# Pacing the first loads of the output projection, and moving operand sums, in a transformer block on one NeuronCore

## The chip, the cores and the metric

The kernel runs on one core of one Trainium2 chip. The metric is the device time of one execution in microseconds. "Before" is the kernel as it stood, "after" the changed one. Single executions of one program scatter by up to 0.6%, so small differences are read from ratios over several rounds and, inside one profile, from the length of stages.

## The reference, cut to what matters

An adaLN modulation is made from `c` and `w_mod`; then an attention block with recurrent memory rows, then an MLP with shifted channels:

```python
mod = (_silu(c) @ w_mod).reshape(c.shape[0], 6, 1, -1)          # sa, ca, ga, sb, cb, gb
h = _layernorm(x) * (1 + ca) + sa
x = x + ga * _A_ref(h, A_mem0, A_Wq, A_Wk, A_Wv, A_Wo, A_seg_len)
h = _layernorm(x) * (1 + cb) + sb
x = x + gb * _B_ref(h, B_w1, B_w2, B_w3, B_w4)
# _A_ref: 32 heads of 128 over 2048 tokens; each segment of 32 tokens sees itself and 8 memory rows;
#         o = p @ v; out = o @ Wo; the memory rows of one segment's output feed the next segment
# _B_ref: u = gelu(layernorm(x) @ w1), shifted along the tokens; x1 = x + shifted @ w2
#         out = x1 + gelu(layernorm(x1) @ w3) @ w4
```

## The kernel before

Six names stand for the engines: in this kernel PE does the matrix products, DVE, ACT and POOL do the element-wise work, and SP, like POOL and ACT, issues DMA transfers. The kernel runs in stages: an **opening** (modulation, first layer norm, means `hbar` of the segments), the **attention** over pairs of heads, the **Wo phase** (`o @ Wo`), the **w1 and w2 tiles**, and twice, for two halves of the tokens ("pairs"), a **w3 stage** and a **w4 stage**. Large products use sums and differences of operand quarters (a fast matrix product with fewer multiplications), made on DVE. A scheduler in the compiler chooses each engine's order; `keep_order` pins an instruction behind the one written before it on that engine.

The eight sums of the opening, free to be placed:

```python
S1, S2, S4 = (hsp.tile([P, 4, CH], F16, name=f"hs{j}{p}")[:] for j in (1, 2, 4))
nc.vector.tensor_tensor(S1, A21, A22, ALU.add)
nc.vector.tensor_tensor(S2, S1, A11, ALU.subtract)
nc.vector.tensor_tensor(S4, A12, S2, ALU.subtract)
nc.vector.tensor_tensor(f16(A21), A11, A21, ALU.subtract)
```

The first loads of the Wo phase, on POOL's queue and on SP's. A unit is 32 matmuls with one 1 MB weight tile (`wstream`) and, on its first use, one 1 MB tile of attention output (`OTc`):

```python
for j in range(1, 3):
    W0_load(0, j, nc.gpsimd)
    load_ot(j, nc.gpsimd)
for t, src in RW:
    nc.gpsimd.dma_start(t[:], src.partition_broadcast(P))
...
interleave(att[done:], ... + W0[0][0] + W0[0][1])
load_ot(3)
...
for j in range(4, 6):
    load_ot(j)
```

The w2 tiles: PE fills a PSUM bank, DVE empties it (`x1b`), ACT takes the squares, three small POOL steps give `ln_ve`, `ln_rstd` and `ln_nmr`, ACT normalises into `z`, and SP transposes `z` into `z2a` or `z2b` by DMA. The sums for w3 stand behind tile 14:

```python
def Bb(t):
    return lambda: nc.sync.dma_start_transpose(z2s[t // 8][:, :, ...], zs[t][:])

for i, u in enumerate(lagged(Ba, Bb, list(range(NTT)), lag=1)):
    u()
    if i in (4, 8):
        load_upto(ring_ctr[0])
    if i == 14:
        for f in z_sums(0):
            keep_order(f())
        w3_sums(0, keep_order)
LT2.close()            # the memory of z, x1b and u is free for what comes next
```

The start of the w3 stage. `snap` copies a bank on ACT, `join` adds a bank and a snap on DVE, `gelu` writes `hq` on ACT. The pools below grow downward into memory that earlier stages gave back:

```python
hq_p = RF.enter_context(tc.tile_pool(name="x3_h", bufs=1, side="right"))
...
st2 = RF.enter_context(tc.tile_pool(name="x3_s2", bufs=2, side="right"))
stm = RF.enter_context(tc.tile_pool(name="x3_sm", bufs=4, side="right"))   # join tiles
rsq = RF.enter_context(tc.tile_pool(name="x3_rq", bufs=2, side="right"))
...
for q in prod("b", A11, B11, True):
    st[q]["s1"] = snap(stA, st[q]["b"])
for q in prod("e", A12, B21, True):
    join(0, 0, q, "e", "s1")
for q in prod("b", S2, T2, False):
    st[q]["s2"] = snap(st2, st[q]["b"])
```

## Time and profile before

| | before |
|---|---|
| time, median of 3 runs | 1491.64 us |
| span of the profile | 1488.7 us |
| PE busy | 1422.2 us, 96% |
| DVE, ACT, POOL busy | 60%, 46%, 25% |

PE is the engine that is always wanted, so the profile is read as a list of PE's waits and of the stretches where its clock is low. A line of the waits is: waiting engine and line, what ended the wait, total us, how often, longest. A line of the order of work ("timeline") is: start in us, duration, engine, line, operation, output<-input, shapes, count, and in brackets the idle time before it with what ended it.

### The profile page before, as it was taken

Reading aid. Unit: us, or ns where it says so; the run is one execution under the profiler, and the core shown is the slowest. Engines: PE = TensorE matmul, PEld = TensorE weight load, DVE = VectorE, ACT = ScalarE, POOL = GpSimd, SP = SyncE. Lnnn points to the kernel's source line nnn. Section 1 sums busy time; section 2 is a strip of 40 time slices with the busy share of each in tenths; the row PEclk is TensorE's granted clock in tenths of the full one; section 3 lists DMA queues with packets and bytes.
Section 4 is the critical chain, followed back from the end, with each engine's and each line's share of the span. In section 5 each row is a group of like instructions: output and inputs, shape, how many; then the busy total and the mean of one; then the engine's idle time right before and its main releaser. Section 6 shows DMA issues by size and latency. Waiting matters only on the chain.

```text
span 1488.7 us, 24706 instructions
## 1 busy us (share of the span) xinstructions
PE 1422.2 (96%) x9198; PEld 754.4 (51%) x9254; DVE 898.1 (60%) x1946; ACT 685.3 (46%) x1443; POOL 379.1 (25%) x530
## 2 busy tenths in 40 slices
PE   5899999999999999999997999999998999999998
PEld 3465555555555555555553444444443444444443
DVE  5517776777677777667651254353255668776684
ACT  2715666665666665666551031122566661046400
POOL 8403100000000000000010132123023557645525
PEclk9999999999999999999999999999999999999999
DMA  9687968867677787778579899994399675387812
GB/s 307 203 284 157 189 155 184 200 146 175 163 175 175 185 165 174 160 163 187 114 178 337 280 319 345 329 261 141 82 311 247 214 249 184 116 248 250 284 39 78
DMA packets 402613, 303.48 MB, mean 204 GB/s; under 512 B 199082, under 2 KB 354730, under 8 KB 400690
## 3 DMA queue, kind: packets, MB, share of 16 engines
q1 hardware_dynamic: 363632, 238.05, 60.8%
q0 software_dynamic: 9616, 33.05, 7.2%
q10 hardware_dynamic: 29234, 30.71, 6.5%
q8 instruction: 74, 1.21, 0.4%
q14 instruction: 57, 0.47, 0.1%
HBM read 200.56 MB, written 50.63 MB: 169 GB/s over the span
## 4 chain that ended last, share of the span: by engine, by line
PE 78%; DMA 5%; DVE 5%; issue 4%; POOL 3%; ACT 3%; ACTq 0%; SPq 0%; DVEq 0%; POOLq 0%
PE acc L623 29%; PE acc L895 7%; PE bank_b L1275 6%; PE bank_b L1224 6%; PE acc L1052 4%; PE acc L328 3%; PE bank_d L1224 3%; PE acc L1151 3%; PE acc L318 3%; PE bank_e L1275 2%; PE bank_d L1275 2%; PE ps_o L734 2%; DMA wstream<-in_A_Wo_dram 2%; PE ps_s L717 2%; PE bank_e L1224 1%
## 5 line engine op out<-in xcount | busy, mean ns | idle before, releaser
L895 PE MATMUL acc<-wstream,OTc 128*128 128x512 bf16 x940 | 209.1, 381 | 6.5 <-DMA OTc<-OTx_d 4.8
L623 PEld LDWEIGHTS <-T 128*128 128x128 f16 x1408 | 130.6, 97 | 119.6 <-issue 2.2
L591 ACT COPY snap<-acc 128x480 f32<-128x480 f32 x264 | 146.3, 565 | 87.3 <-PE acc L623 80.8
L623 PE MATMUL acc<-hh,T 128*128 128x480 bf16 (+1 forms) x704 | 163.1, 366 | 0.3 <-DVE VT L595 0.3
L623 PE MATMUL acc<-hs,T 128*128 128x480 f16 x704 | 157.2, 366 | 0.7 <-ACT snap L591 0.6
L895 PEld LDWEIGHTS <-OTc 128*128 128x128 bf16 x960 | 93.7, 98 | 117.9 <-DMA OTc<-OTx_d 5.0
L762 POOL DMA_DIRECT2D OTx_d<-OT x32 | 24.8, 776 | 427.6 <-DMA OT<-O 368.9
L1224 PEld LDWEIGHTS <-ring 128*128 128x128 f16 (+1 forms) x784 | 77.2, 99 | 104.2 <-issue 12.7
L721 ACT ACTIVATE E<-ps_s 99x495 bf16<-99x495 f32 (+2 forms) x160 | 87.5, 547 | 47.9 <-PE ps_s L717 47.4
L623 PE MATMUL acc<-hh,wq 128*128 128x480 bf16 x464 | 103.9, 366 | 0.0
L741 DVE TENSOR_TENSOR O<-ps_o,rin_all 99x384 bf16<-99x384 f32 (+1 forms) x192 | 97.1, 509 | 3.7
L1078 DVE TENSOR_TENSOR ring<-ring 128x1024 f16<-128x1024 bf16 (+1 forms) x64 | 85.6, 1357 | 5.3 <-PE bank_b L1275 4.8
L1275 PEld LDWEIGHTS <-hq 128*128 128x128 bf16 (+1 forms) x560 | 54.8, 98 | 66.1
L595 DVE TENSOR_TENSOR KT<-acc,snap 128x480 bf16<-128x480 f32 x116 | 74.9, 654 | 21.3 <-PE acc L623 18.7
L734 PE MATMUL ps_o<-V,E 99*128 99x129 bf16 (+1 forms) x704 | 79.8, 220 | 8.1 <-DMA V<-VT 5.5
L1189 ACT COPY snap<-bank_b 128x512 f32<-128x512 f32 x72 | 40.4, 583 | 99.4 <-PE bank_b L1275 60.3
L734 PEld LDWEIGHTS <-E 99*128 99x128 bf16 (+1 forms) x704 | 56.5, 98 | 46.0 <-issue 6.6
L993 ACT ACTIVATE u<-x,ln_nmr,ln_rstd 128x1024 bf16<-128x1024 f32 x16 | 19.7, 1231 | 128.6 <-DVE ln_nmr L992 126.4
L723 DVE TENSOR_TENSOR E<-E,maskB 99x495 bf16<-99x495 bf16 (+1 forms) x128 | 48.2, 376 | 48.4 <-ACT E L721 46.4
L739 ACT ACTIVATE O<-ps_o,rin_all 99x128 bf16<-99x128 f32 x192 | 56.7, 369 | 36.8 <-DVE rin_all L736 36.4
L736 DVE RECIPROCAL rin_all<-ps_o 99x3 f32<-99x3 f32 (+2 forms) x256 | 42.7, 171 | 50.5 <-PE ps_o L734 49.8
L1275 PE MATMUL bank_b<-ring,hq 128*128 128x512 f16 (+1 forms) x334 | 73.1, 379 | 0.1
(245 smaller groups left out, 2549.4 us busy)
## 6 DMA issues: line engine op xcount, KB each, us to landing
wstream<-in_A_Wo_dram SPq DMA_DIRECT2D x29, 1024.0 KB, 9.5
OTx_d<-OT POOLq DMA_DIRECT2D x32, 512.0 KB, 7.0
wstream<-in_B_w_dram SPq DMA_DIRECT2D x28, 512.0 KB, 5.9
ring<-in_B_w_dram SPq DMA_DIRECT2D x28, 512.0 KB, 6.4
ring<-in_B_w_dram SPq DMA_DIRECT2D x8, 1792.0 KB, 10.3
OTc<-OTx_d SPq DMA_DIRECT2D x12, 1024.0 KB, 8.8
wq<-in_A_Wq_dram SPq DMA_DIRECT2D x16, 512.0 KB, 5.1
wk<-in_A_Wk_dram SPq DMA_DIRECT2D x16, 512.0 KB, 8.0
```

The source lines that it names most:

```text
L591: nc.scalar.copy(t[:], st[q][bank][:, 0:CH])
L595: nc.vector.tensor_tensor(view(d, i), chunks(st[q][bank]), chunks(st[q][s_]), ALU.add)
L623: nc.tensor.matmul(acc[:, 0:CH], lhsT=B[:, k, :], rhs=A[:, k, :], start=(j in (1, 2, 5) and k == 0), stop=(k == 3), skip_group_check=True)
L721: nc.scalar.activation(E[:rows, 0:o], ps[:rows, 0:o], ACT.Exp, scale=DH ** -0.5)
L734: nc.tensor.matmul(ps[:, i, :], lhsT=state["e", h, t // 5][:k, c:c + P], rhs=V[:k, t, 0:DH + 1], start=True, stop=True)
L739: nc.scalar.mul(O[:rows, t, :], ps[:rows, i, 0:DH], rin[:, i:i + 1])
L741: nc.vector.tensor_tensor(O[:rows, ts[0]:ts[0] + n, :], ps[:rows, 0:n, 0:DH], rin[:, :, None].to_broadcast([rows, n, DH]), ALU.mult)
L895: nc.tensor.matmul(accs[tt][:], lhsT=ot[hl // 4][:, hl % 4, tt * P:(tt + 1) * P], rhs=woc[hl // 4][:, hl % 4, :], start=(h == 0), stop=(h ...
L1052: nc.tensor.matmul(acc[:], lhsT=w1s[:, kt, ct * P:(ct + 1) * P], rhs=zT[:, kt, b * 512:(b + 1) * 512], start=(kt == 0), stop=(kt == KT - 1))
L1078: return nc.vector.tensor_tensor(dst, a, b, op)
L1224: nc.tensor.matmul(acc[:], lhsT=B[:, k, q * P:(q + 1) * P], rhs=A[:, k, :], start=(start and k == 0), stop=(k == 3), skip_group_check=True)
L1275: nc.tensor.matmul(acc[:], lhsT=L3[:, k, i * P:(i + 1) * P], rhs=R3[:, k, :], start=(start and k == 0), stop=(k == 13), skip_group_check=True)
```

## The change

Its intent is threefold, and I name the parts for the rest of the text.

- **Sums part**: the eight sums of the opening are pinned behind it, off the path to `hbar`.
- **Wo part**: the first loads of the Wo phase go to SP, each released by a named matmul ("paced"); the memory-row transposes of the last two heads go to ACT's queue.
- **z part**: the seven sums in front of the w3 stage are spread, two per w2 tile from tile 10.

```diff
-            nc.vector.tensor_tensor(S1, A21, A22, ALU.add)
+            keep_order(nc.vector.tensor_tensor(S1, A21, A22, ALU.add))
 ... (the same for the other three sums)
+        def pace(ld, mm):
+            if mm is not None:
+                tc.add_manual_dep(ld.ins, mm.ins.name, ...)      # ld waits for matmul mm
 ...
-        for j in range(1, 3):
-            W0_load(0, j, nc.gpsimd)
-            load_ot(j, nc.gpsimd)
-        for t, src in RW:
-            nc.gpsimd.dma_start(t[:], src.partition_broadcast(P))
+        W0_load(0, 1)
+        load_ot(1)
+        paced[0, 0] = [lambda mm: W0_load(0, 2, mm), lambda mm: load_ot(2, mm)]
+        paced[0, 1] = [lambda mm: W0_load(1, 0, mm)]
+        paced[0, 2] = [lambda mm: W0_load(1, 1, mm), ... the row broadcasts RW ...]
+        paced[1, 0] = [lambda mm: W0_load(1, 2, mm), lambda mm: load_ot(3, mm)]
 ... (three more)
         for h in range(H - 2, H):
-            nc.vector.tensor_copy(ots[3][1][:, h % 8 - 4, :], ...)      # moved to a later place
+            nc.scalar.dma_start_transpose(state["mt", h][:], Os[h % 2][96:112, :, :]...)
+            keep_m(h)
 ...
-            if i == 14:
-                for f in z_sums(0):
+            if i == 10:
+                zu = z_sums(0) + w3_sums(0)
+            if i >= 10:
+                for f in zu[2 * (i - 10):2 * (i - 9)]:
                     keep_order(f())
-                w3_sums(0, keep_order)
```

The other edits of the diff, in the w3 and w4 stages, issue the same instructions in the same order.

## The prediction

> **What bounds the kernel now.** I read the page first, then the waits of PE, then the table of stretches around the three longest stalls, then the order of work there on SP and DVE.
>
> ```profile
> PE 1422.2 (96%) x9198; PEld 754.4 (51%) x9254; DVE 898.1 (60%) x1946; ACT 685.3 (46%) x1443; POOL 379.1 (25%) x530
> ```
>
> PE is busy 1422.2 of 1488.7 us. All that a change of order can win is the 66.5 us of PE's idle time, plus whatever PE loses at a lower clock after an idle. So the waits of PE are the list to go by (columns: total us, times, longest):
>
> ```profile
> PE acc L477 <- DVE hbar L465: 5.4, 1, 5.4
> PE bank_b L1224 <- ACT snap L1189: 5.1, 2, 3.2
> PE acc L895 <- DMA OTc<-OTx_d: 4.8, 1, 4.8
> PE acc L895 <- DMA wstream<-in_A_Wo_dram: 4.7, 1, 4.7
> PE bank_b L1224 <- POOL ln_rstd L1135: 4.3, 1, 4.3
> ```
>
> Four of the five lie where the diff works: the hbar wait (opening), both L895 waits (start of the Wo phase), and the last (from the w2 tiles to the w3 stage). The snap waits are not touched: the edits in the w3 and w4 stages issue the same instructions in the same order. The table of stretches (length, busy us by engine, PEclk, DMA share, GB/s) shows what a stall costs beyond itself:
>
> ```profile
> 790.00:794.80 4.80, 0.01 (x1) 0.00 (x0) 0.86 (x3) 0.34 (x1) 0.10 (x1) 1.00 1.00 249
> 794.80:798.50 3.70, 3.65 (x13) 1.63 (x14) 0.00 (x0) 0.00 (x0) 1.68 (x5) 0.55 1.02 389
> 811.60:816.20 4.60, 0.00 (x0) 0.00 (x0) 0.00 (x0) 0.00 (x0) 0.00 (x0) 0.94 1.00 276
> 816.20:818.00 1.80, 1.54 (x4) 0.66 (x6) 0.00 (x0) 0.00 (x0) 0.00 (x0) 0.50 1.27 331
> 1131.00:1135.30 4.30, 0.00 (x0) 0.01 (x1) 4.30 (x7) 2.37 (x3) 1.65 (x4) 0.74 1.05 276
> 1135.30:1141.00 5.70, 5.68 (x16) 2.12 (x17) 1.24 (x4) 4.46 (x6) 1.40 (x4) 0.60 0.92 220
> ```
>
> The stretch after each stall has a granted clock of 0.50 to 0.60. At 1131 PE does nothing while DVE is busy for all 4.30 us. On SP, the order of work around the first two stalls is:
>
> ```profile
> 778.13 0.81 SPq L861 DMA_DIRECT2D OTc<-OTx_d  x2
> 782.49 1.25 SPq L779 DMA_TRANSPOSE MT<-O  x1
> 784.41 0.45 SPq L878 DMA_DIRECT2D wstream<-in_A_Wo_dram  x1
> 784.90 10.21 SPq L861 DMA_DIRECT2D OTc<-OTx_d  x1
> 795.16 1.58 SPq L878 DMA_DIRECT2D wstream<-in_A_Wo_dram  x1
> 801.97 11.89 SPq L779 DMA_TRANSPOSE MT<-O  x1
> ```
>
> The two loads at 778.13 are for later blocks, and at 784.90 and 801.97 SP stands for 10.21 and 11.89 us at one issue. On DVE at the third stall:
>
> ```profile
> 1129.80 0.68 DVE L1153 SCALAR_TENSOR_TENSOR x1b<-acc,u 128x512 f32<-128x512 f32 x1
> ...
> 1133.82 0.69 DVE L1078 TENSOR_TENSOR ring<-ring 128x1024 f16<-128x1024 bf16 x1
> 1134.42 0.68 DVE L1153 SCALAR_TENSOR_TENSOR x1b<-acc,u 128x512 f32<-128x512 f32 x1
> ```
>
> PE's last w2 matmul ends near 1131.0, but its bank is emptied only at 1134.42 (L1153): the operand sums (L1078) stand in front. PE starts w3 at 1135.32, just after that.
>
> **What the Trainium skill says.** (1) "TensorE: Matmul & The Clock Gate", "What's actually happening": after an idle window of about 3.4 us the array runs at half rate, and back at full rate only after about 3.4 us of sustained work. The trace agrees: 8 matmuls after the idle at 790 take 3.35 us, against 1.89 us elsewhere, while the wait of 1.28 us at 123.30 shows no slow matmuls. (2) "DMA: Bandwidth & Descriptors", "Issuing engines are not separate DMA queues": transfers issued from POOL, SP and ACT share the same 16 engines and interleave. The trace agrees: the urgent POOL loads take 16.8 (weights) and 19.4 us (OTc) to land at a DMA share of 1.0, while the weight preloads at 750 (0.5 MB each) landed in 3.3 us. (3) "VectorE: DVE Perf Modes", "The perf-mode tier table": a two-operand bf16 op on 2048 elements takes 1224 ns. The trace has 1218 to 1226 ns (L1078); so 1 us a sum is not to be reduced by order, only moved.
>
> **Part 1, paced Wo loads, transposes off SP.** Before, nearly 10 MB are requested between 778 and 796: for (0,1) and (0,2) 4 MB by POOL; by SP OT 4 and 5 (2 MB), OT 3 (0.75 MB), two weight tiles (2 MB); by POOL the 1 MB of row broadcasts. At some 300 GB/s (stretches: 249 to 389) that is over 30 us, all sharing. What PE needs first at 790 is only 2 MB. After: weight tile 1 and OT 1 go first on SP at about 778 (their memory comes free then, as now), some 2.5 MB with the small loads, so about 8 us, landed by 787, 3 us ahead of 790. Tile 2 and OT 2 start when the first group of 8 matmuls ends (about 783), 2 MB more, due by 793, needed at about 797 (a unit is 32 matmuls of 0.216 us, 6.9 us). The next weight starts near 792, needed at 804. From then each unit brings 1 to 2 MB, with a lead of nearly two units, 12 to 13 us, against a median landing of 9.5 us. So both waits should go.
> - Waits: 4.84 + 4.72 = 9.6 us.
> - Clock: 3.7 x 0.45 = 1.7 us after the first, 1.8 x 0.50 + 22 x 0.02 (PEclk 0.98 from 818 to 840) = 1.3 us after the second.
> - Sum: -12.6 us. The transposes, now on ACT, sit in a stretch with 0.64 us of ACT work in 50 us: no cost on PE's path. PE is busy 49.7 of 50 us in most later stretches, so what is won here carries through, if DMA allows (rivals).
>
> **Part 2, sums over the w2 tiles.** 4 sums of 1.22 us and 3 of 0.69 us move from behind tile 14 to tiles 10 to 13. A tile is 16 matmuls, 3.45 us on PE; DVE's own work in it is 2 x (0.69 + 0.08) + 0.31 = 1.85 us. Six tiles leave 6 x 1.6 = 9.6 us for 7.0 us of sums. The first sum must wait for the last z2a transpose: issued 1111.45, landing 5.1 us (median), 1116.5. DVE then runs late by about 4 us near 1122 and has caught up by tile 15 at about 1130. Eight PSUM tiles give PE 13.8 us of slack meanwhile. The last bank is then emptied from about 1131.1 to 1131.8; PE resumes near 1132.1.
> - Wait 4.3 to 1.1: -3.2 us. Too short to lose the clock: 5.7 x 0.40 = -2.3 us.
> - Given back: ACT has tile 15's normalisation (1.13 and 1.24 us) in front of the first snaps, about +0.5.
> - Sum: -5.0 us.
>
> **Part 3, eight sums behind the opening.** Seven of them (1.15 us each) run now between 63.7 and 71.7 among the steps of hbar, on which PE waits until 73.26. Without them the chain is still held by ACT until 69.43; from there five short steps (0.34 to 0.54 us), 0.15 and 0.20 end at about 72.3: -0.9 us. The wait stays above 3.4 us, so the slow start (0.59 from 73.3 to 79.5) stays. Against it, eight sums at 1.07 us of pitch now stand on DVE from about 114 to 122.7, where the T sums (8 x 0.36 us) and the first masks (at 121.41 now) also want it. The masks may come 3 to 4 us later, when PE has other matmuls for part of that: I put +1.2 us, between 0 and 3. Sum: +0.3 us.
>
> **Total.** -12.6 - 5.0 + 0.3 = -17.3 us; 1491.6 - 17.3 = 1474.3. I hold back about 1 us for new short waits: **1475 us**.
>
> **Rivals.** (a) DMA becomes the bound of the Wo phase: its share is 1.03 to 1.06 from 850 to 1000 at 304 to 343 GB/s. If that is true saturation, PE running 12 us ahead meets loads that land later. For it: the share. Against: no wait on a load in 840 to 1020, 4 weight buffers (20.7 us of lead when not paced) against landings of 9.5 median and 16.7 at most, and a share of 0.40 in 1000 to 1050 that can take deferred stores. It would give back 4 to 10 us: 1479 to 1485. (b) The pacing is too late: a load is released only by a matmul, and a landing of 16.7 us would beat a lead of 13. Each miss costs up to 3 us, perhaps with the clock: 1478 to 1482. (c) The releaser named at 1135, POOL ln_rstd, is the true one and not the emptied bank; it would come only at about 1133, and part 2 wins 3 us instead of 5: 1477. (d) The DVE block at 114 to 123 stalls PE for over 3 us and costs the clock as well: 1479. (e) The hbar chain shortens below 3.4 us, since the compiler's order on ACT changes too: up to 3.5 us more, 1471.
>
> **Range and chances.** Most rivals cost; the two that could add are (e) and smaller waits around 750 to 800. So 1468 to 1484. 2% is 29.8 us, nearly half of all idle time of PE and more than all the touched waits with their clock (19.3 + 7.8 = 27): faster by over 2% 0.03, slower 0.01, within 0.96.
>
> **What would show it.** In the profile after: no L895 wait on OTc or wstream of over 1 us and PEclk 1.0 from 785 to 840; no SP issue that stands for 10 us there; the last L1153 within 1 us of PE's last w2 matmul and PE resuming about 1 us after it at full clock; the hbar wait at about 4.5 us. Wrong would be: new L895 waits after 830 (a or b), a wait on L1135 that stays (c), PE idle in 114 to 130 beyond the present 3 us (d).

## The result, and the profile after

The kernel after takes **1490.25 us** (median of 4 fast runs, 1486.28 to 1491.87) against 1491.89 us for the kernel before beside it (1491.34 to 1493.24). The ratio is 0.9984, with a 95% interval of 0.9963 to 1.0004: the same within 2%. A ratio is the mean time of one kernel's runs over that of the other's of the same rounds, so it is not quite the ratio of the medians quoted. Executions over 1.5% slower than the fastest of the same kernel are left out of the means. The class was predicted, but the time was not: 1475 us was predicted, with 1468 to 1484 as range. About 15 us of gain are missing.

The page of the kernel after, engine totals:

```profile
PE 1423.4 (96%) x9198; PEld 754.6 (51%) x9254; DVE 895.3 (60%) x1946; ACT 685.7 (46%) x1443; POOL 371.8 (25%) x526
```

PE is busy 1.2 us longer, so nothing was won on its idle time either. The waits of PE, after:

```profile
PE bank_b L1244 <- ACT snap L1209: 7.8, 4, 3.4
...
PE acc L477 <- DVE hbar L465: 4.6, 1, 4.6
PE ps_o L734 <- DVE O L741: 4.0, 1, 4.0
PE acc L905 <- DMA OTc<-OTx_d: 3.3, 1, 3.3
PE acc L905 <- DMA wstream<-in_A_Wo_dram: 2.4, 2, 1.8
...
PE bank_b L1244 <- POOL ln_ve L1152: 1.9, 1, 1.9
```

All four waits that the prediction aimed at became shorter: hbar 5.4 to 4.6, the Wo loads 9.5 to 5.7 together, the last one 4.3 to 1.9. But a wait of 4.0 on O is new, and the waits on snap grew from 5.1 to 7.8.

To see where the time went, I measure from the trace when PE starts the first matmul of each stage (of the w2 tiles also the last). The table gives the lengths between these marks in us, for before, after and the four runs that the argument leans on most:

| stretch | before | after | Wo part alone | Wo part, broadcast late | z part alone | best version (best2) |
|---|---|---|---|---|---|---|
| start to the first matmul of L328 (`acc<-hh,wq`, 199 columns) | 113.2 | 111.9 | 112.2 | 112.1 | 112.1 | 112.8 |
| to the first product `hs,wk` | 35.6 | 37.9 | 35.9 | 35.7 | 35.7 | 35.4 |
| rest of the attention | 632.1 | 634.5 | 632.3 | 634.2 | 634.2 | 632.1 |
| Wo phase | 239.4 | 233.0 | 231.2 | 226.5 | 240.0 | 226.5 |
| w1 and w2 tiles | 110.3 | 110.3 | 110.3 | 110.3 | 110.3 | 110.3 |
| last w2 matmul to the first w4 matmul | 93.6 | 94.8 | 95.1 | 95.1 | 94.5 | 87.8 |
| rest | 264.5 | 266.2 | 266.3 | 266.0 | 266.5 | 264.9 |

The z part alone has the same instruction order as before up to the w2 tiles, and yet its attention took 634.2 against 632.1 us: differences of 2 us in that row are scatter of single executions. After won 6.4 us in the Wo phase where 12.6 were predicted, lost 2.3 us in the second row and 1.2 us in the w3 row, and the rest is in rows that scatter.

**The new wait on O.** The order of work on DVE, before:

```profile
123.89 0.56 DVE L741 TENSOR_TENSOR O<-ps_o,rin_all 104x384 bf16<-104x384 f32 x1
...
130.30 0.43 DVE L566 TENSOR_TENSOR T<-wk,wq 128x512 f16<-128x512 bf16 x1 [3.77 <-DMA wk<-in_A_Wk_dram]
```

The same on DVE, after, and then PE, after:

```profile
124.47 0.62 DVE L595 TENSOR_TENSOR VT<-acc,snap 128x480 bf16<-128x480 f32 x1
129.22 0.43 DVE L566 TENSOR_TENSOR T<-wk,wq 128x512 f16<-128x512 bf16 x1 [4.12 <-DMA wk<-in_A_Wk_dram]
...
130.23 0.55 DVE L741 TENSOR_TENSOR O<-ps_o,rin_all 104x384 bf16<-104x384 f32 x1
```

```profile
130.84 0.51 PE L734 MATMUL ps_o<-V,E 99*128 99x129 bf16 x3 [3.96 <-DVE O L741]
```

Both times DVE stands about 4 us for a weight load of the next head pair (L566). Before, the first head's O (L741) had been done by then and nobody waited. After, the pinned sums fill DVE until 123.1 us, the scheduler put L741 behind L566, and PE waits with DVE: the load's delay, hidden before, is now on the path. The wait costs more than its length, since over the next 5 us PE's granted clock is 0.70.

**The Wo phase.** PE's longer waits there, after, then SP and POOL:

```profile
804.60 7.08 PE L905 MATMUL acc<-wstream,OTc 128*128 128x512 bf16 x32 [3.27 <-DMA OTc<-OTx_d]
820.38 16.56 PE L905 MATMUL acc<-wstream,OTc 128*128 128x512 bf16 x74 [1.79 <-DMA wstream<-in_A_Wo_dram]
```

```profile
786.88 2.87 SPq L871 DMA_DIRECT2D OTc<-OTx_d  x1
...
795.59 4.58 SPq L871 DMA_DIRECT2D OTc<-OTx_d  x1
```

```profile
781.47 0.56 POOL L1055 DMA_DIRECT2D gb_b<-rows_d  x1 [6.23 <-PE acc L328]
```

And POOL before:

```profile
796.09 0.54 POOL L1035 DMA_DIRECT2D gb_b<-rows_d  x1
```

The waits at the first use of tile 1 and at 816 us are gone. But one unit later PE waits 3.27 us for tile 2's `OTc`, and two units after that 1.79 us for a weight tile. SP still stands at its issues, though up to 825 us for 4.58 us at most where it stood for 11.89, and a 0.5 MB broadcast, `gb_b`, which is needed only in the w3 stage, is now issued at 781.47 us, in front of most urgent loads; before, it came at 796.09 us, because POOL's queue held its own urgent loads first.

**The start of the w3 stage.** PE after, and then DVE after and DVE before:

```profile
1129.96 1.89 PE L1244 MATMUL bank_b<-z2a,ring 128*128 128x512 bf16 x8 [1.95 <-POOL ln_ve L1152]
1136.93 1.46 PE L1244 MATMUL bank_b<-zs,ring 128*128 128x512 f16 x4 [3.36 <-ACT snap L1209]
1139.39 1.87 PE L1244 MATMUL bank_b<-zs,ring 128*128 128x512 f16 x4 [1.00 <-ACT snap L1209]
...
1313.87 2.62 PE L1244 MATMUL bank_b<-zs,ring 128*128 128x512 f16 x8 [3.25 <-ACT snap L1209]
```

```profile
1142.22 1.29 DVE L1252 TENSOR_TENSOR join<-bank_e,snap 128x512 f32<-128x512 f32 x2 [12.02 <-DMA z2b<-z]
```

```profile
1144.01 1.29 DVE L1232 TENSOR_TENSOR join<-bank_e,snap 128x512 f32<-128x512 f32 x2 [7.43 <-PE bank_d L1224]
```

PE starts w3 at full clock and sooner, as predicted: 2.4 us after its last w2 matmul (1127.6) against 4.7 before (1130.6). Then it waits 3.36 and 1.00 us for snaps. And DVE shows what nobody had asked about: the first join starts 14.6 us after the last w2 matmul, against 13.4 before. Its releaser after is named as a transpose of z, which a join does not read. The profiles of w_only and a_dep, whose code there is that of before, name it too.

### The profile page after: what moved, and what is told of

Same layout as the page of the kernel before. It is cut to its first block, busy times and chain, and to the rows that moved or that the text cites. A ratio compares the mean times of both kernels' runs of the same rounds, so it can differ in the third digit from the quotient of the medians.

```text
span 1488.6 us, 24703 instructions
## 1 busy us (share of the span) xinstructions
PE 1423.4 (96%) x9198; PEld 754.6 (51%) x9254; DVE 895.3 (60%) x1946; ACT 685.7 (46%) x1443; POOL 371.8 (25%) x526
## 5 line engine op out<-in xcount | busy, mean ns | idle before, releaser
L741 DVE TENSOR_TENSOR O<-ps_o,rin_all 99x384 bf16<-99x384 f32 (+1 forms) x192 | 97.1, 509 | 3.7
L595 DVE TENSOR_TENSOR VT<-acc,snap 128x480 bf16<-128x480 f32 x90 | 58.0, 650 | 24.9 <-PE acc L623 20.9
L1248 ACT ACTIVATE hq<-join 128x512 bf16<-128x512 f32 x84 | 52.8, 630 | 41.7 <-DVE join L1252 41.7
```

The costliest lines, as they stand in the source:

```text
L595: nc.vector.tensor_tensor(view(d, i), chunks(st[q][bank]), chunks(st[q][s_]), ALU.add)
L741: nc.vector.tensor_tensor(O[:rows, ts[0]:ts[0] + n, :], ps[:rows, 0:n, 0:DH], rin[:, :, None].to_broadcast([rows, n, DH]), ALU.mult)
L1248: nc.scalar.activation(hq[a][f][:, g * 2 + q, :], src[:], ACT.Gelu_apprx_tanh)
```

## The experiments

Eighteen kernels ran, all correct. They ran with 5 rounds each, in groups that share the runs of the kernel before.

| run | what it is | median us | ratio to before | 95% interval |
|---|---|---|---|---|
| a_only | sums part alone | 1492.06 | 1.0003 | 0.9982 to 1.0023 |
| w_only | Wo part alone | 1483.14 | 0.9935 | 0.9919 to 0.9951 |
| z_only | z part alone | 1492.78 | 1.0002 | 0.9986 to 1.0018 |
| wz | Wo and z parts | 1485.81 | 0.9958 | 0.9938 to 0.9979 |
| w_nomt | Wo part, transposes left on SP | 1481.62 | 0.9939 | 0.9923 to 0.9955 |
| w_mt | only the transposes moved | 1489.86 | 0.9997 | 0.9979 to 1.0014 |
| w_lean | Wo part, gb_b late | 1477.92 | 0.9917 | 0.9900 to 0.9933 |
| a_dep | sums tied behind hbar only | 1491.32 | 1.0006 | 0.9990 to 1.0022 |
| lean_adep | w_lean and a_dep | 1479.59 | 0.9906 | 0.9892 to 0.9920 |
| z_late | z part, tiles 12 to 15 | 1493.20 | 1.0014 | 1.0000 to 1.0027 |
| wz_zact | wz, ACT's normalisation pipelined | 1485.52 | 0.9966 | 0.9951 to 0.9981 |
| z_mem | z_only, join tiles moved | 1504.86 | 1.0099 | 1.0081 to 1.0117 |
| wz_zact_mem | wz_zact, join tiles moved | 1489.76 | 0.9995 | 0.9978 to 1.0013 |
| b_mem2 | before, join tiles moved, POOL pinned | 1490.64 | 0.9985 | 0.9972 to 0.9998 |
| wz_zact_mem2 | wz_zact with the same | 1483.06 | 0.9939 | 0.9921 to 0.9956 |
| best | wz_zact_mem2, gb_b late | 1478.35 | 0.9902 | 0.9888 to 0.9917 |
| best2 | best, addend loads pinned on SP | 1471.17 | 0.9869 | 0.9853 to 0.9886 |
| best2_adep | best2 and a_dep | 1471.48 | 0.9869 | 0.9852 to 0.9885 |

### The parts alone: a_only, w_only, z_only, wz

Each is the kernel before with one part of the diff (wz with two).

> Only the eight operand sums of the opening are kept in order; all else as before. My theory: the sums now fill VectorE after the opening, so the compiler puts O (L741) of the first head behind the T sums of the next pair, which wait for the DMA of wk; PE stands about 4 us for it near 128 us (as in the changed kernel), against some 1.3 us won at hbar and at the clock before 113 us. Expected: 2 us slower than before (some 1494), the wait of ps_o on O in the list of PE's waits at about 4 us. Rival: the stall in the changed kernel came from the timing of that one execution; then this is 1 us faster than before (1491) and the wait is not there.

> Only the Wo part: paced first loads, memory-row transposes off SP. Theory: the stretch is bound by the bytes that PE's order needs there, so of the 12.6 us in the two stalls and their slow clock about half returns as new waits on OTc and wstream of 1 to 4 us: 6 us faster than before (1486). Rival one: in the changed kernel it was hurt by PE coming 3.4 us late; alone it wins all 12 us (1480). Rival two: the win is eaten later by DMA saturation in blocks 1 to 3: 2 us or less (1490), with waits after 840 us.

> Only the spreading of the z and w3 sums over w2 tiles 10 to 13. Theory: PE starts w3 2 to 3 us earlier relative to the end of w2, but then waits for the ScalarE snaps, which stand behind tile 15's normalisation in ScalarE's order; that chain (3.6 us a tile) is not sped up. Net 0 to 2 us faster (1490 to 1492), with snap waits of some 4 us near 1140. Rival: the waits on the snaps came from the earlier parts; then 5 us faster (1487).

> The changed kernel without its kept sums in the opening. Theory: the 4 us stall near 128 us is gone, and the hbar wait is back: 2 to 3 us faster than the changed kernel, some 1487, and about 5 to 6 us faster than before. Rival: the parts do not add up because each gain is lost at the next wait; then equal to the changed kernel, 1490.

Only the Wo part wins: 0.65%, some 9.7 us, where 6 were expected. The sums part and the z part are worth nothing that the intervals show; for the sums part a loss of 2 us had been expected. In a_only's profile the same wait on O of 4.0 us stands as in after; PE is 1.3 us ahead of before at the first matmul of L328 and 1.2 us behind at the first product `hs,wk`. So the parts, not their meeting, explain most of the missing gain. A remainder is left: the three ratios multiply to 0.9940, and the whole change has 0.9984. Of this, wz over w_only is 0.0023 and after over wz is 0.0026. The four parts ran in one group of rounds and the whole change in another, and the intervals of wz and w_only overlap, as do those of after and wz. In the profiles wz is only 0.4 us longer than w_only, and after is 4.9 us longer than wz: 1.1 us in the first two rows together, 1.6 in the attention, which scatters, and 2.0 in the Wo phase. No single wait accounts for it; it stays open.

### Which half of the Wo part: w_nomt, w_mt

```diff
 w_nomt = w_only
+            if c == 2:
+                nc.sync.dma_start_transpose(state["mt", h][:], O[96:112, :, :]...)     # in its turn on SP, as before
 w_mt = before
-            if c == 2:
-                nc.sync.dma_start_transpose(state["mt", h][:], O[96:112, :, :]...)
+        for h in range(H - 2, H):                                                # behind W0[0][2], on ACT
+            nc.scalar.dma_start_transpose(state["mt", h][:], Os[h % 2][96:112, :, :]...)
+            keep_m(h)
```

> Only the paced Wo loads, the memory-row transposes stay on SP in their turns. Whole Wo part alone gave 0.9935. Theory 'pacing carries the gain' (urgent loads share with fewer others): 0.994 to 0.995, the wait at the first load near 790 gone, the wait after 804 below 3 us. Theory 'the transposes carry it' (SP stood behind them): the ratio stays at 0.998 or above and SP again stands for 5 us or more at an issue behind a transpose between 778 and 815, with a PE wait on wstream or OTc of over 3 us.

> Only the transposes moved to ACT's queue with the split of keep, loads as before (POOL). Theory 'pacing carries the gain': ratio 0.998 to 1.001, waits of 4 to 5 us at 790 and near 811 remain. Theory 'the transposes carry it': ratio 0.994 to 0.996, both waits below 2 us.

The paced loads carry all of it (0.9939), the move of the transposes nothing (0.9997). Not separated is what the pacing consists of: the loads moved from POOL to SP and were tied to matmuls at once, and no run did one without the other. SP in w_mt, where no transpose stands in its way any more:

```profile
781.57 12.91 SPq L865 DMA_DIRECT2D OTc<-OTx_d  x1
794.52 17.20 SPq L882 DMA_DIRECT2D wstream<-in_A_Wo_dram  x2
```

SP stands for 12.91 us, and for 17.20 us at two issues, all the same, at a DMA share of 1.01 and 1.04. So the transposes were not what made SP stand. In w_only, where fewer bytes are asked for together, no issue on SP between 777 and 815 us stands for more than 3.77 us, which fits the bytes as the cause.

### What was left of the Wo waits: w_lean

In w_only one wait is left, and it costs more than its length:

```profile
799.83 8.77 PE L905 MATMUL acc<-wstream,OTc 128*128 128x512 bf16 x32 [2.33 <-DMA OTc<-OTx_d]
```

The 32 matmuls behind the 2.33 us take 8.77 us; after's take 7.08 us behind a longer wait. The edit makes only the broadcast wait:

```diff
-                nc.gpsimd.dma_start(gb_b[:], rows_d[1].partition_broadcast(P))
+                pace(nc.gpsimd.dma_start(gb_b[:], rows_d[1].partition_broadcast(P)), first_mm[1, 3])
```

> The Wo part alone with the 0.5 MB broadcast of gb_b (issued at 777 us, needed only in the w3 stage) released by a late matmul of the Wo phase. Theory 'the first units are bound by bytes (each 6.9 us unit wants 2 MB, 300 GB/s at a DMA share of 1.0, so 0.5 MB costs 1.6 us)': the OTc wait falls from 2.3 us to below 1 us and the total by 1 to 2 us against the Wo part alone. Rival 'it is the lead of the release, 14 us against a landing of 14 to 16 us, whatever the bytes': wait unchanged, total the same within 0.5 us.

In w_lean the broadcast is issued at 836.29 us, no wait on OTc or wstream is left between 780 and 1020 us, and the Wo phase takes 226.5 us against 231.2. The table of stretches (length, PE, PEld, DVE, ACT, POOL busy, PEclk, DMA share, GB/s), w_only and then w_lean:

```profile
795.00:800.00 5.00, 2.67 (x18) 1.17 (x17) 0.00 (x0) 0.64 (x1) 0.75 (x1) 1.00 1.06 361
800.00:805.00 5.00, 5.00 (x17) 1.92 (x16) 2.50 (x5) 0.00 (x0) 2.21 (x6) 0.66 0.88 315
```

```profile
795.00:800.00 5.00, 4.95 (x34) 2.52 (x33) 0.92 (x3) 0.64 (x1) 0.75 (x1) 1.00 0.97 333
800.00:805.00 5.00, 5.00 (x25) 2.28 (x24) 0.89 (x3) 0.00 (x0) 1.11 (x4) 1.00 1.03 237
```

The wait and the clock of 0.66 behind it are both gone. The ratios of w_only and w_lean differ by about 2.7 us where 1 to 2 were expected, but their intervals overlap, so the gain is read from the stage. There it repeats: with `gb_b` late the Wo phase takes 226.5 to 227.6 us in all five profiles (w_lean, lean_adep, best, best2, best2_adep), with the Wo part and `gb_b` early 230.3 to 233.0 in all seven. The bytes theory holds: a unit needs 2 MB in 6.9 us, some 304 GB/s, and DMA moved 237 to 389 GB/s here at a share near 1.0, so 0.5 MB in front of it is a wait.

### Where the sums should stand: a_dep, lean_adep

```diff
+        def after_hbar(ins):
+            tc.add_manual_dep(ins.ins, gs["last"].ins.name, ... NoSync ...)    # behind hbar's last step, nothing more
-            nc.vector.tensor_tensor(S1, A21, A22, ALU.add)
+            after_hbar(nc.vector.tensor_tensor(S1, A21, A22, ALU.add))
 ... (the same for the other three sums)
```

> The eight sums alone, placed behind hbar's last step only, not pinned behind the whole opening. The sums part alone gave 1.0003: it won 1.3 to 1.8 us up to 113 us and lost more than that by 137 us, where DVE stood for a weight load with the first head's O product behind it (PE wait of 4.0 us on O). Theory 'the place behind the opening cost it, not the move off hbar's path': hbar wait about 4.6 instead of 5.4 us, no PE wait on O of over 1 us at 127 to 137, total 1 to 1.5 us below before (ratio 0.999). Rival 'the sums cost the same wherever they go': ratio 1.000 or above and a new wait elsewhere between 73 and 137 us.

> w_lean with the eight sums tied behind hbar's last step. a_dep alone was 2.5 us ahead of before at 780 us and only 1.2 us ahead at 1020 us, with the waits for Wo's transfers unchanged in end but longer by what PE came earlier. Theory 'transfers took it back': with no wait on transfers left, the gain carries through, 1 to 2.5 us below w_lean (1477.9), so about 1476. Rival 'DMA is now the bound of the stage': new OTc or wstream waits of 1 to 2.5 us and the total of w_lean.

In a_dep's profile the hbar wait is 4.6 us and the wait on O is gone; PE there:

```profile
120.96 0.33 PE L737 MATMUL ps_o<-V,E 104*128 104x129 bf16 x3 [1.36 <-DMA V<-VT]
130.39 0.34 PE L737 MATMUL ps_o<-V,E 99*128 99x129 bf16 x3 [0.39 <-DVE E L726]
```

PE is 2.5 us ahead of before at the first product `hs,wk`, so the place behind the opening was the cost. But the total does not show it: 1.0006. I had taken it that Wo's transfers took the lead back. The trace of a_dep says no: its two waits there are 4.8 and 5.0 us, as in before, and start as much sooner as PE does. The lead was lost to the clock: the 29 matmuls behind the second wait take 8.50 us there and 7.19 us in before, and another 1.4 us went in the "rest" row. PE in a_dep, and then in before:

```profile
815.00 8.50 PE L898 MATMUL acc<-wstream,pre_o 128*128 128x512 bf16 x29 [0.22 <-issue]
```

```profile
817.49 7.19 PE L895 MATMUL acc<-wstream,pre_o 128*128 128x512 bf16 x29 [0.22 <-issue]
```

In the joined run, lean_adep is 1.8 us ahead of w_lean at the first w3 matmul and 0.6 us behind it at the first w4 matmul, after waits for snaps of 0.5, 1.4 and 2.5 us. Its ratio is 0.9906 against 0.9917 for w_lean, but its median is higher by 1.7 us, and the intervals overlap. best2_adep has exactly the ratio of best2, as its rival said. So the sums' gain stands in the one profile of the stage and is not shown in the total; at 1 to 2 us it is of the size of the scatter.

### Why the z part won nothing, first try: z_late, wz_zact

In z_only the first sum waits for the last transposes of z2a (3.09 us on DVE at 1119.66 us), so z_late issues the sums two tiles later. wz_zact takes away ACT's idle time instead: it normalises tile t behind the squares of tile t+1.

```diff
 z_late = z_only
-            if i == 10:
+            if i == 12:                         # and the slices counted from 12
 wz_zact = wz
-            nc.scalar.activation(dst, src, ACT.Identity, bias=nmr[:], scale=rstd[:])
+            return lambda: keep_order(nc.scalar.activation(dst, src, ACT.Identity, bias=nmr[:], scale=rstd[:]))
...
+            if 1 <= i <= NTT:
+                norms[i - 1]()                  # the transposes of z follow one tile later, too
```

> The z part alone, with its seven sums two tiles later (tiles 12 to 15 in place of 10 to 13). Theory 'the first sum waits 3.1 us for the z2a transposes, delays DVE and through ln_nm the ACT chain': that DVE wait falls below 1 us, the last normalisation and the first snaps come 2 to 3 us sooner, the span from the last w2 matmul to the first of the w3 stage's second group shrinks by 2 us, total 1490 to 1491 against 1492.8 for the z part. Rival 'ACT's own serial chain of 3.58 us a tile sets it whatever DVE does': snap wait unchanged at about 3.4 us and total within 0.5 us of the z part; or, third, the sums are now again ahead of the last evacuations and the old 4.3 us wait on the bank returns in part.

> Wo part and z part together, with the normalisation of tile t put on ACT behind the squares of tile t+1, so ACT does not stand idle for POOL's three small steps. Theory 'ACT's serial chain puts the snaps of w3 late': ACT's pace falls from 3.58 to about 2.4 us a tile, the snap waits (3.4 and 1.0 us near 1133) go, clock stays at 1.0 there, and the total is about 3 to 4 us below the run of both parts (1485.8), so about 1482. Rival 'the snap wait is set by DVE or PSUM': the same waits, total within 1 us of 1485.8.

z_late's sums stand later without the stop for z2a, and the total is no better (1.0014). ACT in z_late shows why:

```profile
1131.25 1.24 ACT L1137 ACTIVATE z<-x1b,ln_nmr,ln_rstd 128x1024 bf16<-128x1024 f32 x1 [1.22 <-POOL ln_nmr L1136]
...
1134.83 1.24 ACT L1137 ACTIVATE z<-x1b,ln_nmr,ln_rstd 128x1024 bf16<-128x1024 f32 x1 [1.21 <-POOL ln_nmr L1136]
```

A tile takes 3.58 us there (1134.83 − 1131.25), and 1.2 us of it ACT waits for POOL's three small steps. PE makes a tile in 3.45 us, so ACT falls behind, and the first snaps stand in ACT's list behind the last tiles. wz_zact brings ACT to 2.3 us a tile, and PE indeed passes the first group sooner, but not the second. PE and DVE in wz_zact:

```profile
1122.70 1.89 PE L1251 MATMUL bank_b<-z2a,ring 128*128 128x512 bf16 x8 [0.94 <-POOL ln_ve L1152]
...
1127.51 1.89 PE L1251 MATMUL bank_b<-zs,ring 128*128 128x512 f16 x8 [1.20 <-ACT snap L1216]
...
1136.97 3.57 PE L1251 MATMUL bank_b<-zs,ring 128*128 128x512 f16 x8 [5.85 <-ACT snap L1216]
```

```profile
1134.49 1.29 DVE L1259 TENSOR_TENSOR join<-bank_e,snap 128x512 f32<-128x512 f32 x2 [11.55 <-DMA z2b<-z]
```

PE's waits of 3.36 and 1.00 us have become one of 5.85 us, and 8 matmuls take 3.57 us behind it. My theory, that ACT alone was the hold, fell: the total is 1485.5 us, where 1482 was expected, and the ratio of 0.9966 is no better than the 0.9958 of wz. Over all runs so far the first join starts between 13.1 and 14.6 us after the last w2 matmul, whatever stood before it. The addresses in the built program say why a join waits for a transpose of z: the four join tiles lie on bytes 118752 to 126944 of each partition, the last four z tiles on 119616 to 127808. A join may not write there before the transposes have read z, and in the program built from the kernel before the first join does wait for the semaphores that the last four transposes count up.

### The memory under the join: z_mem, wz_zact_mem

```diff
-        hq_p = RF.enter_context(tc.tile_pool(name="x3_h", bufs=1, side="right"))
 ... (the other pools, which so move up)
         rsq = RF.enter_context(tc.tile_pool(name="x3_rq", bufs=2, side="right"))
+        hq_p = RF.enter_context(tc.tile_pool(name="x3_h", bufs=1, side="right"))
 ... (the four hq tiles are made in another order)
```

> The z part alone, with the join tiles of the w3 stage in other memory: until now they lie on the memory of the last z tiles, so the first join must wait until the last transpose of z has landed (in every run so far the first join starts 13.1 to 14.6 us after the last w2 matmul, whatever PE did before). Theory 'that memory sets the start of w3': the first join no longer names DMA z2b, starts at most 11.5 us after the last w2 matmul (14.3 in the z part alone), and the total falls by 2 to 4 us below the z part alone, to a ratio of about 0.998. Rival 'ACT's normalisations set it': the join starts as late as before, total unchanged within 1 us.

> Both holds of the w3 start taken away at once: ACT's pipelined normalisation and the join tiles off the memory of z (with the Wo and z parts). ACT alone left the total at 1485.5, because the join still waited for z2b until 13.1 us after the last w2 matmul. Theory 'two holds in series': first join about 6 to 7 us after the last w2 matmul, the 5.8 us snap wait gone, no slow clock there, total 7 to 9 us below the run without the memory move, about 1477 (ratio 0.991). Rival 'something third (ring loads, z2a sums) holds it as well': less than 3 us.

The step that was tested came true in z_mem: the join waits for its snap and starts 9.1 us after the last w2 matmul (1131.1). But both kernels got slower (1.0099 against 1.0002 for z_only, 0.9995 against 0.9966 for wz_zact). DVE and then ACT in z_mem:

```profile
1140.27 1.29 DVE L1233 TENSOR_TENSOR join<-bank_e,snap 128x512 f32<-128x512 f32 x2 [6.70 <-ACT snap L1189]
```

```profile
1149.20 1.24 ACT L1137 ACTIVATE z<-x1b,ln_nmr,ln_rstd 128x1024 bf16<-128x1024 f32 x1 [8.48 <-POOL ln_nmr L1136]
1155.51 1.15 ACT L1229 ACTIVATE hq<-join 128x512 bf16<-128x512 f32 x2 [5.06 <-DMA z2b<-z]
```

Two new holds, both my doing. The scheduler was now free to put POOL's addend products, which wait for loads, in front of the last tile's three steps, so ACT waits 8.48 us for `ln_nmr`. And the pool of hq now covers z's memory, and its first tile waited for the transposes.

### Mended: b_mem2, wz_zact_mem2, best

```diff
+        hq_pA = RF.enter_context(tc.tile_pool(name="x3_hA", bufs=1, side="right"))     # hq11, hq00: used first
+        hq_pB = RF.enter_context(tc.tile_pool(name="x3_hB", bufs=1, side="right"))     # hq10, hq01: on z's memory
...
-                    nc.gpsimd.tensor_tensor(xb[:], xb[:], gb_b[:, cs], ALU.mult)
+                    mul = nc.gpsimd.tensor_tensor(xb[:], xb[:], gb_b[:, cs], ALU.mult)
+                    tc.add_manual_dep(mul.ins, last_ln["nmr"].ins.name, ... NoSync ...)
 best = wz_zact_mem2 with the gb_b edit of w_lean
```

> The kernel before, with only the memory move of the join tiles (and of hq) and POOL's addends pinned behind the last normalisation. Theory 'the first join waits for the last z2b transpose because it lies on z's memory': first join at about 10.6 us after the last w2 matmul (right behind the second snap) in place of 13.4, the later PE wait of 1.9 us on a snap gone, total 2 to 3 us below before (ratio 0.998 to 0.9985). Rival 'the join is held by PE or ACT anyway': join at 13.4 us, ratio 1.000.

> Wo and z parts with both holds mended: pipelined normalisation on ACT, join tiles and first hq tiles off z's memory, addends behind the last normalisation on POOL. Theory 'two holds in series': first join about 6.5 us after the last w2 matmul (13.1 with ACT alone), PE waits on snaps before the second pair below 1.5 us, clock 1.0 throughout, total 6 to 9 us below wz_zact (1485.5), so 1477 to 1479. Rival 'a third hold': join early but a new PE wait of over 3 us within the first two groups of the w3 stage, on DVE sums, hq or a ring load; total above 1482.

> wz_zact_mem2 with the broadcast of gb_b released late. If both hold: the Wo stage as in w_lean (3.5 us better than the Wo part alone) and the w3 start as in wz_zact_mem2, in sum 1472 to 1475 (ratio 0.988 to 0.990). If the w3 start is held by a third thing: no better than w_lean, 1478.

b_mem2 is the kernel before with these two edits, to the memory and to POOL's order. DVE in it:

```profile
1140.12 0.69 DVE L1237 TENSOR_TENSOR join<-bank_e,snap 128x512 f32<-128x512 f32 x1 [3.13 <-PE bank_e L1229]
1141.54 0.69 DVE L1237 TENSOR_TENSOR join<-bank_e,snap 128x512 f32<-128x512 f32 x1 [0.73 <-ACT snap L1192]
```

The joins now follow PE and ACT, at 9.1 and 10.5 us after the last w2 matmul (1131.0) in place of 13.4, and the stretch from the last w2 matmul to the first w4 matmul falls from 93.6 to 91.0 us. In the eight kernels with the code of before there (before among them) that stretch takes 93.5 to 97.5 us. The ratio of 0.9985 is what was expected, with an interval that ends just below 1 (0.9998). So the memory hold is shown in the kernel before, read from the start of the join; POOL's pin came with it and was not run alone. wz_zact_mem2 has the join 6.4 us after the last w2 matmul, but its total is 1483.06: the theory (1477 to 1479) missed, and the rival came true, a third hold with a total above 1482 and a PE wait of over 3 us (3.55 us, for a snap at 1144.25). ACT names the hold:

```profile
1141.60 1.15 ACT L1260 ACTIVATE hq<-join 128x512 bf16<-128x512 f32 x2 [6.35 <-DMA z2b<-z]
```

This is the hq tile that I had to leave on z's memory. The last two transposes are issued only from 1132.47 us on, behind addend and ring loads on SP. best missed its 1472 to 1475 us in the same way: 1478.35, as its rival said, and 0.9902 against 0.9917 for w_lean, with overlapping intervals. ACT waits 6.41 us for z2b there.

### The last hold: best2, best2_adep

```diff
+                last_ln["tr"] = nc.sync.dma_start_transpose(z2s[t // 8][...], zs[t][:])
...
-                    nc.sync.dma_start(xb[:], x1b_d[rows, cs])
+                    ld = nc.sync.dma_start(xb[:], x1b_d[rows, cs])
+                    tc.add_manual_dep(ld.ins, last_ln["tr"].ins.name, ... NoSync ...)
```

> best (1478.35, ratio 0.9902) with the addend loads on SP pinned behind the last z2b transpose. Theory 'the remaining PE wait of 3.6 us on a snap at the second group of the w3 stage comes from transposes issued behind those loads': ACT's wait on z2b falls from 6.4 to about 2 us, PE's from 3.6 to below 1 us with no slow clock, total 3 to 5 us lower, about 1474 (ratio 0.987). Rival 'the transposes land no sooner, since each is issued only when the one before has landed or DMA is full': unchanged.

> best2 with the eight sums tied behind hbar's last step. In the profiles of w_lean and lean_adep the gain at the end of the Wo phase was 1.7 us. Theory 'it carries through when nothing waits on transfers': 1 to 2 us below best2, ratio 0.986. Rival: same as best2 within 0.5 us, with the gain lost at the w3 start or the second pair.

best2 takes 1471.17 us (1470.79 to 1471.64), a ratio of 0.9869: 1.3% faster than before, below the 1474 expected, and better than both kernels that the diff compares. Its interval lies apart from that of best, and ACT's wait for z2b is gone, so the order on SP was the last of the three holds. PE in best2, and one line of best2_adep:

```profile
1118.49 1.89 PE L1261 MATMUL bank_b<-z2a,ring 128*128 128x512 bf16 x8 [1.04 <-issue]
...
1123.72 1.89 PE L1261 MATMUL bank_b<-zs,ring 128*128 128x512 f16 x8 [1.62 <-ACT snap L1223]
...
1296.85 1.89 PE L1261 MATMUL bank_b<-zs,ring 128*128 128x512 f16 x8 [3.25 <-ACT snap L1223]
```

```profile
1297.60 3.37 PE L1264 MATMUL bank_b<-zs,ring 128*128 128x512 f16 x8 [3.25 <-ACT snap L1226]
```

Two short waits are left at the start of the w3 stage, the clock stays at full rate, and the stretch takes 87.8 us where before took 93.6. The last line of best2 and that of best2_adep are the same wait, in the second pair, 3.25 us long in both; 8 matmuls behind it take 1.89 us in one and 3.37 us in the other. In all 20 profiles that wait is 3.24 or 3.25 us. The clock held in 6 of them (before, a_only, w_mt, z_late, wz_zact_mem2, best2) and fell in 14. That splits the "rest" row: it takes 264.3 to 264.9 us in those 6 and 265.9 to 266.7 us in the 14.

## Why the prediction was wrong, point by point

Predicted were -12.6 us from part 1, -5.0 from part 2 and +0.3 from part 3. The profiles of before and after show -6.4 us in the Wo phase, +1.2 at the start of w3 and +1.0 in the first two rows; the attention (+2.4) and the rest (+1.7), which scatter from execution to execution, take what was left.

- **Part 1, "So both waits should go"**: the two waits did go, and the transposes cost nothing, as said. The step that failed is the list of bytes that stand before PE's need. It counted the weight tiles, OT 1 and small loads, and put the row broadcasts behind a late matmul; it left out that `gb_b` (0.5 MB), once POOL's queue was empty, would move up to 777 to 781 us. That left a wait of 2.3 us with 1.7 us of slow clock in w_only (8.77 us less the 7.08 us of the same 32 matmuls in after), and 3.3 and 2.4 us in after, which was not itself run with `gb_b` late. With `gb_b` late the Wo phase falls by 12.9 us (239.4 to 226.5), where 12.6 were predicted: mechanism and size of the rest were right. One more 1 MB `OTc` load was overlooked: SP has four of them at 778 to 785 us in the prediction's own lines, 3.75 MB and not 2.75, and one of the pair at 778.13 is tile 3, of the first block and not of a later one. One of the four (tile 6 by elimination, of the next block) has no release in the changed kernel; w_lean still issues it (793.28 us) and has no wait, so it was not what was missing.
- **Rival (a), DMA as the bound**: half right. From 840 to 1020 us after has only one wait on a load, of 0.62 us, but the first three units are bound by bytes. Rival (b), a pacing too late, came true in its sign (waits of up to 3.3 us) but not in its cause: w_lean has the same pacing, less to load, and no wait.
- **Part 2, "Wait 4.3 to 1.1: -3.2 us"**: the wait did shrink (1.95 in after, 1.67 in z_only), so the emptied bank was its cause and rival (c) fell: a releaser on POOL is still named, but the wait followed the bank, which is emptied at 1129.75 us in after, 0.2 us before PE starts. The step that failed is that what is won there is won in the end. Behind this wait stood two others that would have come due at the same moment: ACT's normalisations at 3.58 us a tile, with the snaps behind them, and the join on z's memory. "Given back ... about +0.5" should have been all of it. To win it took four more edits, to ACT's order, POOL's, SP's and to memory; with them the stretch is 5.8 us shorter. That this is near the 5.0 predicted is luck, since it came by other steps.
- **"Too short to lose the clock: -2.3 us"**: true at this wait, but by luck, and wrong as a rule. PE lost the clock behind waits of 1.95 us (w_nomt, 8.77 us for 32 matmuls) and 2.33 us (w_only), and kept it behind 3.27 us (after). Over all 20 profiles, of PE's waits that began at full clock none of up to 1.88 us was followed by a slow clock, every one from 3.35 us on was, and between 1.94 and 3.27 us both came. After, it was lost at the next wait, 3.36 us for a snap.
- **Part 3**: the hbar term was right (4.6 us measured, about 4.5 predicted). The slow start stayed, but its size is not fixed: in the 6.2 us behind the wait the clock is 0.59 in before, 0.78 in after, and 0.52 to 0.78 over all 20 profiles. The block on DVE was taken as a delay of 3 to 4 us "when PE has other matmuls for part of that". What it did was change the order: O went behind an instruction that waits for a load, and PE waited 3.96 us and lost the clock. That is rival (d), with another mechanism than a full DVE; it stood among the rivals and should have been in the sum.
- **"What is won here carries through, if DMA allows"**: in the Wo phase it did (w_lean's 12.9 us are still 11.8 us at the last w2 matmul, since its Wo phase had begun 1.1 us later). At the start of w3 it did not, and the limit was not DMA's rate but the order and the memory there.
- **The range** left no room for the chance that two of three parts give nothing.

## What to carry to other kernels

Before you count a removed wait as won, ask of each engine and each buffer in that stage what would be the next to hold PE, and when it comes due: read the order on ACT and DVE for the first instruction of the next stage, and look whether its tile lies on memory that a transfer still reads. Where you pin one instruction, the scheduler moves others; look for an instruction that waits for a transfer and now stands in front of work that PE needs. In a stage at a DMA share near 1.0, list every load with its size and time of issue, also those that nobody needs yet, since emptying a queue lets them move up.

## What the Trainium skill lacked or had wrong

- "TensorE: Matmul & The Clock Gate", "What's actually happening", ties the half rate to at least one idle window of about 3.4 us. Here, of PE's waits that began at full clock, none of up to 1.88 us was followed by the slow clock and every one from 3.35 us on was, but between 1.94 and 3.27 us both came: slow behind 1.95 and 2.33 us (8.77 us for 32 matmuls in place of 7.08), full behind 3.27 us, and one wait of 3.24 to 3.25 us went slow in 14 of 20 profiles. The section calls the window free-running, which fits an outcome that varies; that 1.95 us can be enough does not follow from it. As a threshold for predictions, "shorter than 3.4 us costs no clock" is wrong in this case.
- "Perfetto Trace Analysis", "Optimization Strategy", says to find what blocks an engine's gap by the semaphore or semaphores it waits on and the instruction that updates them. Nothing there warns that the one releaser a profile names can hide another that is about as late: the join is put down to PE's bank_d in before (7.43 us idle) and, with the same code there, to the transposes of z in w_only (7.31 us idle), and moving its memory (b_mem2: 13.4 to 9.1 us behind the last w2 matmul) settled it.
- "DMA: Bandwidth & Descriptors", "Issuing engines are not separate DMA queues", is borne out: moving transposes from SP to ACT changed nothing (0.9997), taking 0.5 MB away from the same stretch did (the Wo phase fell from 231.2 to 226.5 us). What no page has is how long an issue stands when the engines are full: 12.91 us, and 17.20 us for two, on SP in w_mt.
